# Tiled bias attention and a cosine-gated FFN: q and k transposed once in fp32, split into high and low halves afterwards

## The chip, the core and the metric

One core of a Trainium2 chip runs the whole program. The metric is device time in microseconds (us), the median of several executions. Engines are named as in the profile: PE is TensorE's matmul row and PEld its weight loads, DVE is VectorE, ACT is ScalarE, POOL is GpSimd, SP is SyncE, whose queue issues all DMAs.

## The reference

```python
scores = scale * np.matmul(q, k.transpose(0, 1, 3, 2))        # B=4, H=8, S=576, D=64
scores = scores + bias.transpose(2, 0, 1)[None]               # bias: a small MLP of log distances, per head
scores = scores - np.max(scores, axis=-1, keepdims=True)
attn = np.exp(scores); attn = attn / (attn.sum(-1, keepdims=True) + 1e-9)
x = np.matmul(attn, v)                                        # then (B*S, H*D) = (2304, 512)
h = x @ w_in; g = h * np.cos(h); out = g @ w_out              # d_ff = 2048
```

All is fp32. Products that need it are made of three fp32r matmuls, for which a matrix is split into a rounded high half and the low half that is left: high x high, high x low and low x high.

## The kernel before, in words

The program has three stages. The **bias stage** (to about 65 us) makes 36 groups of bias rows (`bias_hid`, `bias_rows`, `bias_store`) and stores them to DRAM, from where `load_bias` (L226) reads them back in tiles per head. The **attention stage** (to about 365 us) treats 16 units, a unit being a pair of heads of one batch element. The **FFN stage** takes the rest.

Order is written out by hand: `manual_schedule` keeps each engine's instructions in the order in which the Python code emits them, and the semaphores follow from the data. So an instruction that waits holds up all behind it on its engine.

A unit has five **slots** (`slot`, L551), one for each tile of 128 query rows (the fifth holds the last 64 rows of both heads). Slot j of a unit emits the scores of its tile (`qk`, L397: 12 fp32r matmuls, 6 in the fifth), for which two PSUM tiles (`ps_s`, two buffers, one for each head) are taken; DVE adds the bias and takes the minimum in one instruction (L419). The exponentials of the slot before are done on ACT (L437), their sums inverted on DVE (L449, L452) and the rows scaled by POOL (`norm`, L459). The tile of three slots ago is transposed on PE (L466, eight transposes; L471, one for the 64 left columns) and copied out of PSUM by ACT (first head) and DVE (second head). V's matmuls (`pv`, L514) of the unit before run in slots 0, 1, 3 and 4; their result is copied by ACT (L479) in slots 1 and 4.

**q and k of the next unit** are prepared beside that. `load` (L141) brings a pair of heads with one DMA for 512 rows (four successive rows, 1 KB, to a partition) and for k two more with the 64 rows left of k and of q. `split` (L169) makes the halves on POOL: one instruction for the high half (L176) and two for the low one (L179). `turn_main` (L188) transposes one half with four fp32r transposes (L191) into a PSUM bank and copies it on ACT (L198); `turn_left` (L205) does the 64 rows left of both halves with two transposes (L208) and four ACT copies (L211, L213). `T_EARLY` (L545) places them: k high in slot 0, k low in slot 1, the left rows and q high in slot 2, q low in slot 3, each between the scores and V's matmuls. All transposes take banks from one ring of three (`ps_t`, L380): a bank can be written again when the copy of what it held three requests ago is done. `POOL_PLAN` (L538) places the splits behind the norms of a slot, a unit or two ahead; `LOAD_PLAN` (L547) the loads; `W_PLAN` (L548) the FFN weights' conversion, a part of it in each second unit (DVE's L105 in slot 1, POOL's L109 in slot 2). For unit 0 the same is done in the bias stage (`T_FIRST`, L351, and the splits at n == 1).

Of the kernel before, what the change touches and what calls it, by code (L numbers as in the profile page):

```python
# [28 lines left out]
def kernel(  # L29
# [81 lines left out]
    with tc.manual_schedule():  # L111
# [21 lines left out]
        for t_ in qDs:  # L133
            nc.vector.memset(f(t_[0:64, :, 64:128]), 0.0)
            nc.vector.memset(f(t_[64:128, :, 0:64]), 0.0)

        vN = [vl.tile([128, 9, D], F32, name=f"vN{i}") for i in range(2)]

# [2 lines left out]
        def load(u, x):  # L141
            hp, b = units[u]
            src = {"q": q, "k": k, "v": v}[x]
            pair_ = src[b, 2 * hp : 2 * hp + 2]
            if x == "v":
                t = vN[u % 2]
                for h in range(2):
                    nc.sync.dma_start(
                        out=t[:, 4 * h : 4 * h + 4, :], in_=pair_[h, 0:512].rearrange("(c p) d -> p c d", p=128)
                    )  # L150
                for h in range(2):
                    nc.sync.dma_start(out=t[64 * h : 64 * h + 64, 8, :], in_=pair_[h, 512:576])
                return
            m = 5 if x == "k" else 4
            t = (lk if x == "k" else ld).tile([128, 2, m, D], F32, tag=x, name=f"n{x}")
            nc.sync.dma_start(
                out=t[:, :, 0:4].rearrange("p h r d -> p h (r d)"),
                in_=pair_[:, 0:512].rearrange("h (p r) d -> p h (r d)", r=4),
            )
            if x == "k":  # L160
                for i, o in ((k, 0), (q, 64)):
                    nc.sync.dma_start(
                        out=t[o : o + 64, :, 4], in_=i[b, 2 * hp : 2 * hp + 2, 512:576].rearrange("h p d -> p h d")
                    )
            nat[u, x] = t

        spl = {}

        def split(u, x, step=None):  # L169
            n = nat[u, x]  # L170
            m = n.shape[2]
            if step in (None, 0):
                spl[u, x] = sp.tile([128, 2, m, 128], F32R, tag=x, name=f"s{x}")
            hi, lo = (spl[u, x][:, a].rearrange("p c (h d) -> p h c d", h=2) for a in range(2))
            if step in (None, 0):
                nc.gpsimd.tensor_scalar(hi, n, 1.0, 1.0, ALU.mult, ALU.mult)  # L176
            for h in range(2):
                if step in (None, 1 + h):
                    nc.gpsimd.tensor_tensor(lo[:, h], n[:, h], f(hi[:, h]), ALU.subtract)  # L179
            if step in (None, 2):  # L180
                nat.pop((u, x))

        kN = {}

        def bank(dt=F32):
            return ps_t.tile([128, 512], dt, tag="t", name="pt")

        def turn_main(u, x, a):  # L188
            ps = bank(F32R)
            for c in range(4):  # L190
                nc.tensor.transpose(ps[:, 128 * c : 128 * c + 128], spl[u, x][:, a, c], identr)  # L191
            if x == "q":
                o = qTs[u % 2][:, a]
            else:
                if u not in kN:
                    kN[u] = tp.tile([128, 2, 640], F32R, tag="kN", name="kN")
                o = kN[u][:, a, 64:576]
            nc.scalar.activation(  # L198
                out=o.rearrange("p (x c) -> p x c", c=4),
                in_=f(ps).rearrange("p (c x) -> p x c", c=4),  # L200
                func=AF.Copy,
                scale=-0.125 if x == "q" else 1.0,
            )

        def turn_left(u):  # L205
            ps = bank(F32R)
            for a in range(2):
                nc.tensor.transpose(ps[:, 128 * a : 128 * a + 128], spl[u, "k"][:, a, 4], identr)  # L208
            i = f(ps)[:, 0:256].rearrange("p (a x) -> p a x", a=2)
            for o in (576, 0):  # L210
                nc.scalar.activation(out=kN[u][:, :, o : o + 64], in_=i[:, :, 0:64], func=AF.Copy)  # L211
            for r in (slice(0, 64), slice(64, 128)):
                nc.scalar.activation(out=qDs[u % 2][r, :, r], in_=i[r, :, 64:128], func=AF.Copy, scale=-0.125)  # L213

        def turn(u, ops):
            if u >= NU:
                return
            for op in ops:
                if op == "kx":
                    turn_left(u)  # L220
                else:
                    turn_main(u, op[0], "hl".index(op[1]))

        bias = {}

# [122 lines left out]
        for i in range(WPRE):  # L348
            W[i] = wpre[i]
        ACT_H = [k for k in range(36) if k % 4 != 3]  # L350
        T_FIRST = {11: ("kh",), 12: ("kl",), 13: ("kx",), 14: ("qh",), 15: ("ql",)}  # L351
        todo = [(t, gi) for t in (4, 0, 1, 2, 3) for gi in range(len(groups[t]))]
        held, hts = None, bias_hid(0)
        for n in range(len(todo) + 1):
            now = hts
            if n < len(todo):
                hts = bias_hid(n + 1) if n + 1 < len(todo) else None
                ps = bias_rows(n, now)
            if held:
# [6 lines left out]
            if n == 1:  # L366
                for x in "kq":
                    split(0, x)
            if n == 6:
                for x in "kq":  # L370
                    load(1, x)
            if n in T_FIRST:
                turn(0, T_FIRST[n])
            if n == 16:
                split(1, "k")
            if n == 20:
                load(2, "k")
        stage.close()
# [18 lines left out]
        def qk(u, j):  # L397
# [3 lines left out]
            for hf in range(2):  # L401
                for n, (a, b) in enumerate(((0, 0), (0, 1), (1, 0))):
                    for h in heads:
                        r = slice(64 * h, 64 * h + 64) if t < 4 else slice(0, 128)
                        o = HALF * hf + (64 if h == 0 else 0)
                        nc.tensor.matmul(  # L406
                            s[h][:, hf, 0:HALF],
                            qTs[u % 2][r, a, 128 * t : 128 * t + 128] if t < 4 else qDs[u % 2][:, a],
                            kN[u][r, b, o : o + HALF],
                            start=(n == 0),  # L410
                            stop=(n == 2),
                            tile_position=(r.start, 0),
                        )
# [100 lines left out]
        def pv(u, hf, chunks):  # L514
# [5 lines left out]
            for c in chunks:  # L520
                for h in range(2):
# [11 lines left out]
            if 4 in chunks:  # L533
                c0 = b * S + 256 * hf
                act_copy(xT[:, hp, c0 : c0 + WQ[hf]], X_.pop((u, hf))[:, 0 : WQ[hf]])
# [12 lines left out]
        W_PLAN = [("abs", 2), (0, 3), (0.5, 4), (1, 5), (2, 6), ("load", 6), (3, 7), (4, 7)]  # L548
        get = lambda i: jobs[i] if 0 <= i < len(jobs) else None

        def slot(i):  # L551
# [3 lines left out]
            if now:  # L555
                qk(u, j)
            if last:
                softmax_exp(*last, 0)
            turn(u + 1, T_EARLY[j])
            if last and len(heads(last)) == 2:  # L560
                softmax_exp(*last, 1)
            for du, hf, chunks in PV_EARLY[j]:
                if 0 <= u + du < NU:
                    pv(u + du, hf, chunks)
            if prev:
                if prev[1] in (0, 2):
                    alloc_half(prev[0], prev[1] // 2)
# [5 lines left out]
            if prev:  # L573
# [2 lines left out]
                    keep_main(*prev, 1, pt[1])  # L576
                else:
                    keep_both(prev[0], pt[0])
            if last:
                for h in heads(last):  # L580
                    norm(*last, h)
            if prev:
                keep_left(*prev, pl)
            if now:
                for du, x, step in POOL_PLAN[j]:
                    if u + du < NU:
                        split(u + du, x, step)
# [244 lines left out]
```

## Time and profile before

| | |
|---|---|
| time, median of 3 runs (lowest to highest) | 783.94 us (783.48 to 785.31) |
| profiled execution: time / span of its instructions | 785.39 us / 783.6 us |
| PE busy | 755.1 us, 96% |
| PEld busy | 603.7 us, 77% |
| DVE busy | 599.4 us, 76% |
| ACT busy | 465.4 us, 59% |
| POOL busy | 395.3 us, 50% |
| DMA | 58.57 MB in 58825 packets, 24.3% of 16 engines' span |

The busy shares are averages over three stages with different limits. The page's table of 40 slices shows PE at nine tenths or more nearly everywhere except in the first four slices (the bias stage and its end), and PE's granted clock at nine tenths or more but there. So the stage in which the change lies must be read slot by slot.

### The profile page before, as it was taken

The numbers are of one execution on the slowest core, as the hardware profiler recorded it, in microseconds if no ns is written. First come the engines' busy times: TensorE is split into PE (matmuls) and PEld (weight loads), VectorE is DVE, ScalarE is ACT, GpSimd is POOL, SyncE is SP. The second block draws the span as 40 slices with busy tenths as digits, with TensorE's granted clock in tenths as the row PEclk, the third lists the DMA queues.
The fourth block names the chain that finished last, engine by engine and source line by source line (L and its number), as shares of the span: only waits on it lengthen the run. The fifth ranks groups of instructions, "written<-read, shape, count | busy, mean of one in ns | idle before, by whom it ended". The sixth has DMA issues, their size and how long they took to land.

```text
span 783.6 us, 14808 instructions
## 1 busy us (share of the span) xinstructions
PE 755.1 (96%) x5338; PEld 603.7 (77%) x5338; DVE 599.4 (76%) x1309; ACT 465.4 (59%) x964; POOL 395.3 (50%) x486
## 2 busy tenths in 40 slices
PE   6988899999999999998999999999999999999997
PEld 2665676667666667666798989988888889899895
DVE  8973768687777777775468878899889898976655
ACT  5975677777777777785355555545454545443332
POOL 2201566676767666657345537455455464554400
PEclk9995899999999999999999999999999999999999
DMA  5775314422533161120010101111110101001112
GB/s 184 249 253 188 98 48 135 121 78 56 166 91 89 49 191 49 28 61 11 1 54 28 55 28 54 32 50 31 50 53 30 54 27 55 2 28 41 54 41 81
DMA packets 58825, 58.57 MB, mean 75 GB/s; under 512 B 28544, under 2 KB 45056, under 8 KB 58752
## 3 DMA queue, kind: packets, MB, share of 16 engines
q1 hardware_dynamic: 58752, 57.63, 24.3%
q8 instruction: 42, 0.69, 0.4%
q14 instruction: 31, 0.25, 0.1%
HBM read 42.00 MB, written 15.61 MB: 74 GB/s over the span
## 4 chain that ended last, share of the span: by engine, by line
PE 85%; DVE 6%; DMA 4%; ACT 2%; issue 2%; SPq 0%; DVEq 0%; ACTq 0%
PE ph L634 25%; PE po L689 24%; PE pv L524 12%; PE s L406 9%; PE pt L466 8%; PE pa L323 3%; PE pt L191 3%; DMA sc<-rt 2%; DVE P L419 1%; DVE ht L307 1%; PE pt L471 1%; DMA bt<-sc 1%; DVE PT L482 1%; DVE gl L663 1%; DVE acc L712 0%
## 5 line engine op out<-in xcount | busy, mean ns | idle before, releaser
L459 POOL TENSOR_SCALAR P<-P,rc 128x576 f32<-128x576 f32 x144 | 107.3, 756 | 112.7 <-ACT P L437 40.5
L638 ACT ACTIVATE a<-ph,quarter 128x384 int32<-128x384 f32 x96 | 55.6, 580 | 107.8 <-PE ph L634 107.0
L419 DVE CUSTOM_DVE_ANT_0 P<-s,bt 128x576 f32<-128x576 f32 x144 | 103.5, 751 | 20.6 <-PE s L406 13.7
L644 DVE SCALAR_TENSOR_TENSOR r<-a,ph 128x384 f32<-128x384 int32 x96 | 52.8, 550 | 79.5 <-ACT a L638 79.4
L437 ACT ACTIVATE P<-P,m 128x576 f32<-128x576 f32 x144 | 110.8, 771 | 2.6 <-DVE m L419 2.6
L509 POOL TENSOR_TENSOR xs<-xT,xs 128x384 fp32r<-128x384 f32 x96 | 107.2, 1116 | 8.0
L634 PE MATMUL ph<-xs,wpre 128*128 128x384 f32 x576 | 109.4, 338 | 0.8 <-DVE a L653 0.8
L634 PE MATMUL ph<-xs,w 128*128 128x384 f32 x576 | 108.3, 337 | 0.5 <-DVE a L653 0.5
L634 PEld LDWEIGHTS ph<-xs,wpre 128*128 128x128 f32 x576 | 101.8, 188 | 6.5 <-DVE a L653 2.1
L634 PEld LDWEIGHTS ph<-xs,w 128*128 128x128 f32 x576 | 101.4, 188 | 5.5 <-DVE a L653 1.4
L649 ACT ACTIVATE r<-r,hpi 128x384 f32<-128x384 f32 x96 | 59.3, 617 | 69.6 <-DVE r L645 69.6
L508 POOL TENSOR_SCALAR xs<-xT 128x384 fp32r<-128x384 f32 x96 | 61.6, 641 | 48.7 <-PE ph L634 48.7
L466 PEld LDWEIGHTS pt<-ident,P 128*128 128x128 f32 x576 | 62.9, 143 | 29.7 <-POOL P L459 13.7
L466 PE MATMUL pt<-ident,P 128*128 128x128 f32 x576 | 81.5, 283 | 2.3 <-DVE PT L482 2.3
L524 PE MATMUL pv<-PT,vN 128*64 128x320 f32 (+1 forms) x512 | 77.8, 424 | 2.6 <-ACT PT L479 2.4
L406 PE MATMUL s<-kN,qT 64*128 64x288 f32 x768 | 77.0, 323 | 2.8 <-DVE m L419 1.4
L689 PE MATMUL po<-w,gh 128*128 128x512 f32 x288 | 75.3, 396 | 0.0
L689 PE MATMUL po<-wpre,gh 128*128 128x512 f32 x288 | 75.2, 396 | 0.0
L663 DVE TENSOR_TENSOR gl<-a,gh 128x384 fp32r<-128x384 f32 x96 | 74.0, 771 | 0.6 <-ACT gh L657 0.6
L406 PEld LDWEIGHTS s<-kN,qT 64*128 64x128 f32 x768 | 59.0, 195 | 15.6 <-issue 7.5
L482 DVE COPY PT<-pt 128x512 f32<-128x512 f32 x64 | 43.9, 686 | 33.5 <-PE pt L466 33.5
L109 POOL TENSOR_TENSOR w<-wb,w 128x512 fp32r<-128x512 f32 x16 | 20.7, 1295 | 89.9 <-ACT w L107 89.9
(82 smaller groups left out, 1300.6 us busy)
## 6 DMA issues: line engine op xcount, KB each, us to landing
sc<-rt SPq DMA_DIRECT2D x36, 295.5 KB
raw<-in_moe_w_in_dram SPq DMA_DIRECT2D x16, 512.0 KB
raw<-in_moe_w_out_dram SPq DMA_DIRECT2D x16, 512.0 KB
bt<-sc SPq DMA_DIRECT2D x16, 288.0 KB
nk<-in_k_dram SPq DMA_DIRECT2D x16, 256.0 KB
nq<-in_q_dram SPq DMA_DIRECT2D x16, 256.0 KB
vN<-in_v_dram SPq DMA_DIRECT2D x32, 128.0 KB
bt<-sc SPq DMA_DIRECT2D x16, 256.0 KB
```

The source lines that it names most:

```text
L406: nc.tensor.matmul(s[h][:, hf, 0:HALF], qTs[u % 2][r, a, 128 * t : 128 * t + 128] if t < 4 else qDs[u % 2][:, a], kN[u][r, b, o : o + HALF ...
L419: nc.vector.tensor_tensor_reduce(neg.rearrange("p (a x) -> p a x", a=2), s[h][:, :, 0:HALF], bias[hp, t, h].rearrange("p (a x) -> p a x", ...
L437: nc.scalar.activation(out=P[u, j][:, 576 * h : 576 * h + 576], in_=neg, func=AF.Exp, bias=m[:, 0:1], scale=-1.0, accum_out=dn[u, j][:, h ...
L459: nc.gpsimd.tensor_scalar(p, p, r, 1.0, ALU.mult, ALU.mult)
L466: nc.tensor.transpose(ps[:, 128 * c : 128 * c + 128], p[:, o : o + 128], ident)
L508: nc.gpsimd.tensor_scalar(h, src, 1.0, 1.0, ALU.mult, ALU.mult)
L509: nc.gpsimd.tensor_tensor(l, src, f(h), ALU.subtract)
L524: nc.tensor.matmul(ps[64 * h : 64 * h + 64, 0 : WQ[hf]], a, m, start=(c == 0), stop=(c == 4), tile_position=(r.start, 64 * h), skip_group_ ...
L634: nc.tensor.matmul(ps, a, x, start=(i == 0), stop=(i == 3 * KD - 1))
L649: nc.scalar.activation(out=r, in_=r, func=AF.Sin, scale=SIN_SCALE, bias=hpi)
L663: nc.vector.tensor_tensor(gl, a, f(G[key][0]), ALU.subtract)
L689: nc.tensor.matmul(O[n][i], a[:, 128 * i : 128 * i + 128], w, start=(i0 == 0 and p == 0), stop=(i0 == GF - 1 and p == 2),)
```

## The change

- k and q are transposed as loaded, in fp32: four transposes and one ACT copy for each (512 rows), and one transpose with four copies for the 64 rows left of both. The copies go to SBUF tiles `turned["k"]` and `turned["q"]` of 640 columns; q is scaled and the two left blocks lie at columns 512 to 639 of q, with zeros beside them that are written once.
- POOL splits those: for each of k and q a high half of 640 columns (step 0) and two low halves of 320 columns (steps 1 and 2), written to where the scores read them. It follows the transposes, where it was ahead of them.
- The order in a slot: scores, both exponentials of the slot before, V's matmuls and ACT's copy of their result, the q/k transposes and their copies, P's transposes. k is turned in slot 0, the left rows in slot 1, q in slot 2. Splits come in slots 2 (k: steps 0 and 1 ahead of the norms, 2 behind), 3 (q: 0 ahead, 1 behind) and 4 (q: 2 ahead of the norms).
- The loads of q and k take one DMA for each head, and lay four rows of a head at a distance of two heads' width, so that the pieces are 256 bytes. q's load buffer is doubled, and the split halves' pool is gone; q is loaded two units ahead in slot 0, k three ahead in slot 2.
- For unit 0, k, the left rows and q are turned at n = 11, 12, 13 of the bias stage and split at 13 and 14; unit 1's k is split in unit 0's slots.

```diff
-        ld = opened(front, "ld", 1, "right")
+        ld = opened(front, "ld", 2, "right")
-        sp = opened(front, "sp", 1, "right")
...
-        qTs = [st.tile([128, 2, 512], F32R, name=f"qT{i}") for i in range(2)]
-        qDs = [st.tile([128, 2, 128], F32R, name=f"qD{i}") for i in range(2)]
...
+        qTs = [st.tile([128, 2, 640], F32R, name=f"qT{i}") for i in range(2)]
+        turned = {x: st.tile([128, 640], F32, name=f"{x}t") for x in "kq"}
...
-            t = (lk if x == "k" else ld).tile([128, 2, m, D], F32, tag=x, name=f"n{x}")
-            nc.sync.dma_start(
-                out=t[:, :, 0:4].rearrange("p h r d -> p h (r d)"),
-                in_=pair_[:, 0:512].rearrange("h (p r) d -> p h (r d)", r=4),
-            )
+            t = (lk if x == "k" else ld).tile([128, m, 2, D], F32, tag=x, name=f"n{x}")
+            for h in range(2):
+                nc.sync.dma_start(out=t[:, 0:4, h], in_=pair_[h, 0:512].rearrange("(p r) d -> p r d", r=4))
...
         def split(u, x, step=None):
+            n = turned[x]
...
             if step in (None, 0):
+                nc.gpsimd.tensor_scalar(o[:, 0], n, 1.0, 1.0, ALU.mult, ALU.mult)
+            for i in range(2):
+                c = slice(320 * i, 320 * i + 320)
+                if step in (None, 1 + i):
+                    nc.gpsimd.tensor_tensor(o[:, 1, c], n[:, c], f(o[:, 0, c]), ALU.subtract)
...
-                nc.tensor.transpose(ps[:, 128 * c : 128 * c + 128], spl[u, x][:, a, c], identr)
+                nc.tensor.transpose(ps[:, 128 * c : 128 * c + 128], n[:, c], ident)
...
+        def keep_turned(x, ps):
+            if x == "x":
+                o = turned["k"]
+                for at in (0, 576):
+                    nc.scalar.activation(out=o[:, at : at + 64], in_=ps[:, 0:64], func=AF.Copy)
+                for h in range(2):
+                    r = slice(64 * h, 64 * h + 64)
+                    nc.scalar.activation(
+                        out=turned["q"][r, 512 + 64 * h : 576 + 64 * h], in_=ps[r, 64:128], func=AF.Copy, scale=-0.125
+                    )
+                return
...
-        T_FIRST = {11: ("kh",), 12: ("kl",), 13: ("kx",), 14: ("qh",), 15: ("ql",)}
+        T_FIRST = {11: "k", 12: "x", 13: "q"}
+        S_FIRST = {13: "k", 14: "q"}
...
-            [(1, "q", 0), (1, "q", 1), (1, "q", 2)],
-            [],
-            [(2, "k", 0)],
-            [(2, "k", 1)],
-            [(2, "k", 2)],
+            ([], []),
+            ([], []),
+            ([("k", 0), ("k", 1)], [("k", 2)]),
+            ([("q", 0)], [("q", 1)]),
+            ([("q", 2)], []),
...
-        T_EARLY = [["kh"], ["kl"], ["kx", "qh"], ["ql"], []]
+        T_EARLY = ["k", "x", "q", None, None]
-        LOAD_PLAN = [[(3, "k")], [(2, "q")], [], [], [(1, "v")]]
+        LOAD_PLAN = [[(2, "q")], [], [(3, "k")], [], [(1, "v")]]
...
             if last:
-                softmax_exp(*last, 0)
-            turn(u + 1, T_EARLY[j])
-            if last and len(heads(last)) == 2:
-                softmax_exp(*last, 1)
+                for h in heads(last):
+                    softmax_exp(*last, h)
             for du, hf, chunks in PV_EARLY[j]:
                 if 0 <= u + du < NU:
                     pv(u + du, hf, chunks)
+                    if 4 in chunks:
+                        keep_x(u + du, hf)
+            if T_EARLY[j] and u + 1 < NU:
+                keep_turned(T_EARLY[j], turn(u + 1, T_EARLY[j]))
...
+            for x, step in POOL_PLAN[j][0]:
+                if u + 1 < NU:
+                    split(u + 1, x, step)
             if last:
                 for h in heads(last):
                     norm(*last, h)
             if prev:
                 keep_left(*prev, pl)
+            for x, step in POOL_PLAN[j][1]:
+                if u + 1 < NU:
+                    split(u + 1, x, step)
```

## Rows read from the trace of the kernel before

**Rows 1.** Stretches: us, busy us (count) of PE, PEld, DVE, ACT, POOL; PEclk, DMA share, GB/s.

```profile
40.00:65.00 25.00, 19.81 (x359) 12.76 (x350) 15.56 (x45) 16.91 (x26) 0.00 (x0) 0.88 0.78 265
...
100.00:150.00 50.00, 49.43 (x421) 34.35 (x419) 37.18 (x109) 37.13 (x92) 34.07 (x47) 1.00 0.41 118
```

**Rows 2.** PE's timeline of unit 4: start us, length us, engine, line, what, count.

```profile
139.91 1.05 PE L406 MATMUL s<-kN,qT 64*128 64x288 f32 x12
...
142.37 1.10 PE L466 MATMUL pt<-ident,P 128*128 128x128 f32 x8
...
143.51 1.06 PE L406 MATMUL s<-kN,qT 64*128 64x288 f32 x12
144.50 0.54 PE L191 MATMUL pt<-identr,sk 128*128 128x128 f32 x4
144.97 1.08 PE L524 MATMUL pv<-PT,vN 128*64 128x256 f32 x8
...
146.57 1.09 PE L466 MATMUL pt<-ident,P 128*128 128x128 f32 x8
...
147.70 1.06 PE L406 MATMUL s<-kN,qT 64*128 64x288 f32 x12
148.69 0.36 PE L208 MATMUL pt<-identr,sk 128*128 128x128 f32 x2
...
149.24 0.62 PE L466 MATMUL pt<-ident,P 128*128 128x128 f32 x4
150.03 0.33 PE L471 MATMUL pt<-ident,P 128*128 128x128 f32 x1 [0.16 <-ACT qD L213]
150.28 1.17 PE L406 MATMUL s<-kN,qT 64*128 64x288 f32 x12
151.38 0.54 PE L191 MATMUL pt<-identr,sq 128*128 128x128 f32 x4
151.89 1.30 PE L524 MATMUL pv<-PT,vN 128*64 128x320 f32 x8
...
154.08 1.03 PE L406 MATMUL s<-kN,qD 128*128 128x288 f32 x6
...
158.08 0.79 PE L406 MATMUL s<-kN,qT 64*128 64x288 f32 x8
```

**Rows 3.** ACT's timeline in slots 1 and 2 of unit 4.

```profile
146.71 0.38 ACT L479 ACTIVATE xT<-pv 128x256 f32<-128x256 f32 x1 [0.28 <-PE pv L524]
...
149.09 0.45 ACT L211 ACTIVATE kN<-pt 128x128 fp32r<-128x128 f32 x2 [0.48 <-PE pt L208]
...
150.00 0.60 ACT L198 ACTIVATE qT<-pt 128x512 fp32r<-128x512 f32 x1
```

**Rows 4.** DVE's timeline in slot 2 of unit 4: the second head's bias and minimum.

```profile
149.57 0.75 DVE L419 CUSTOM_DVE_ANT_0 P<-s,bt 128x576 f32<-128x576 f32 x1
```

**Rows 5.** The timeline of unit 3, slot 3: PE's weight load for the second head's scores.

```profile
132.26 0.82 PEld L406 LDWEIGHTS s<-kN,qT 64*128 64x128 f32 x11 [0.34 <-DVE m L419]
```

**Rows 6.** Groups by line and form on POOL, 100 to 340 us: busy us, mean ns | idle before.

```profile
L459 POOL TENSOR_SCALAR P<-P,rc 128x576 f32<-128x576 f32 x119 | 88.6, 756 | 63.9 <-PE pt L191 24.1 <-PE s L406 18.4 <-DVE rc L452 7.9
L179 POOL TENSOR_TENSOR sk<-nk,sk 128x320 fp32r<-128x320 f32 x26 | 23.5, 903 | 0.0
...
L109 POOL TENSOR_TENSOR wpre<-wb,wpre 128x512 fp32r<-128x512 f32 x7 | 9.0, 1293 | 0.0
L176 POOL TENSOR_SCALAR sk<-nk 128x640 fp32r<-128x640 f32 x12 | 8.7, 729 | 0.0
```

**Rows 7.** The timeline where unit 0 ends and unit 1 begins, POOL and PE.

```profile
82.22 1.63 POOL L459 TENSOR_SCALAR P<-P,rc 128x576 f32<-128x576 f32 x2 [3.26 <-DVE rc L452]
...
84.02 1.81 PE L406 MATMUL s<-kN,qT 64*128 64x288 f32 x12
```

**Rows 8.** Stretches as in rows 1: V's load lies in the first, q's in the second.

```profile
304.00:309.00 5.00, 5.00 (x48) 3.90 (x49) 4.00 (x12) 3.17 (x7) 3.40 (x6) 1.00 0.27 59
...
313.00:318.00 5.00, 4.72 (x45) 3.49 (x45) 4.29 (x14) 4.49 (x13) 1.92 (x4) 1.00 0.20 52
```

More of the change, by code (lines that the diff above doesn't have):

```diff
@@ L130 @@
         nc.vector.tensor_copy(identr, ident)
-        qTs = [st.tile([128, 2, 512], F32R, name=f"qT{i}") for i in range(2)]
-        qDs = [st.tile([128, 2, 128], F32R, name=f"qD{i}") for i in range(2)]
-        for t_ in qDs:
-            nc.vector.memset(f(t_[0:64, :, 64:128]), 0.0)
-            nc.vector.memset(f(t_[64:128, :, 0:64]), 0.0)
+        qTs = [st.tile([128, 2, 640], F32R, name=f"qT{i}") for i in range(2)]
+        turned = {x: st.tile([128, 640], F32, name=f"{x}t") for x in "kq"}
+        nc.vector.memset(turned["q"][0:64, 576:640], 0.0)
+        nc.vector.memset(turned["q"][64:128, 512:576], 0.0)
         vN = [vl.tile([128, 9, D], F32, name=f"vN{i}") for i in range(2)]
@@ L162, in load @@
                     nc.sync.dma_start(
-                        out=t[o : o + 64, :, 4], in_=i[b, 2 * hp : 2 * hp + 2, 512:576].rearrange("h p d -> p h d")
+                        out=t[o : o + 64, 4], in_=i[b, 2 * hp : 2 * hp + 2, 512:576].rearrange("h p d -> p h d")
                     )
             nat[u, x] = t
-        spl = {}
         def split(u, x, step=None):
-            n = nat[u, x]
-            m = n.shape[2]
-            if step in (None, 0):
[L173 to L181, printed above, removed]
+            n = turned[x]
+            if x == "k":
+                if u not in kN:
+                    kN[u] = tp.tile([128, 2, 640], F32R, tag="kN", name="kN")
+                o = kN[u]
+            else:
+                o = qTs[u % 2]
+            if step in (None, 0):
+                nc.gpsimd.tensor_scalar(o[:, 0], n, 1.0, 1.0, ALU.mult, ALU.mult)
[3 more added lines that the diff above has]
+                    nc.gpsimd.tensor_tensor(o[:, 1, c], n[:, c], f(o[:, 0, c]), ALU.subtract)
         kN = {}
@@ L186, in bank, with turn_main, turn_left @@
             return ps_t.tile([128, 512], dt, tag="t", name="pt")
-        def turn_main(u, x, a):
-            ps = bank(F32R)
+        def turn_main(u, x):
+            ps = bank()
+            n = nat[u, x].rearrange("p r h d -> p r (h d)")
             for c in range(4):
-                nc.tensor.transpose(ps[:, 128 * c : 128 * c + 128], spl[u, x][:, a, c], identr)
[L192 to L197, printed above, removed]
+                nc.tensor.transpose(ps[:, 128 * c : 128 * c + 128], n[:, c], ident)
+            return ps
+        def turn_left(u):
+            ps = bank()
+            nc.tensor.transpose(ps[:, 0:128], nat[u, "k"][:, 4].rearrange("p h d -> p (h d)"), ident)
+            return ps
+        def keep_turned(x, ps):
[9 more added lines that the diff above has]
+                return
+            o = turned[x][:, 64:576] if x == "k" else turned[x][:, 0:512]
             nc.scalar.activation(
                 out=o.rearrange("p (x c) -> p x c", c=4),
-                in_=f(ps).rearrange("p (c x) -> p x c", c=4),
+                in_=ps.rearrange("p (c x) -> p x c", c=4),
                 func=AF.Copy,
@@ L203, in turn_main, with turn @@
             )
[L205 to L222, printed above, removed]
+        def turn(u, x):
+            return turn_left(u) if x == "x" else turn_main(u, x)
         bias = {}
@@ L365 @@
             held = (n, ps)
-            if n == 1:
-                for x in "kq":
-                    split(0, x)
             if n == 6:
@@ L372 @@
             if n in T_FIRST:
-                turn(0, T_FIRST[n])
-            if n == 16:
-                split(1, "k")
+                keep_turned(T_FIRST[n], turn(0, T_FIRST[n]))
+            if n in S_FIRST:
+                split(0, S_FIRST[n])
             if n == 20:
@@ L407, in qk @@
                             s[h][:, hf, 0:HALF],
-                            qTs[u % 2][r, a, 128 * t : 128 * t + 128] if t < 4 else qDs[u % 2][:, a],
+                            qTs[u % 2][r, a, 128 * t : 128 * t + 128] if t < 4 else qTs[u % 2][:, a, 512:640],
                             kN[u][r, b, o : o + HALF],
@@ L583, in slot @@
                 keep_left(*prev, pl)
+            for x, step in POOL_PLAN[j][1]:
+                if u + 1 < NU:
+                    split(u + 1, x, step)
             if now:
-                for du, x, step in POOL_PLAN[j]:
-                    if u + du < NU:
-                        split(u + du, x, step)
                 for du, x in LOAD_PLAN[j]:
```

7 lines of the change are left out of this document (4 added, 3 removed).

## The prediction, made before the changed kernel ran

> **What bounds the kernel now.** I read the stretches first. From 100 to 340 us, over four such stretches, PE is busy in 99% of the time at full clock while DVE and ACT lie near 75% and POOL at 68% [rows 1]: PE sets the pace of the attention stage, and this is where q and k are turned. From 40 to 65 us PE has 19.8 of 25 us and DMA a share of 0.78 [rows 1]; there the chain of waits goes through stores to and loads from DRAM, so nothing is won there from a shorter PE. The FFN stage is untouched.
>
> Then I read PE's order in one unit [rows 2], since a busy PE can hide waits. Its slots start at 139.91, 143.51, 147.70, 150.28, 154.08 and 158.08: 3.60, 4.19, 2.58, 3.80, 4.00, in sum 18.17 us. Units with an even number repeat this; odd ones take 18.54, with all the difference in slot 3, where the second head's scores wait 0.34 for DVE [rows 5]. Unit 0 is held by DMAs and unit 15 turns nothing, so 14 units count.
>
> **The change part by part.** *The q/k transposes.* From the start of a group to the next group, k high and k low take 144.97 - 144.50 = 0.47 each, the left rows and q high 149.24 - 148.69 = 0.55, q low 151.89 - 151.38 = 0.51 [rows 2]: 2.00 us in a unit, of which a part is the switch to V's matmuls. A run of nine fp32 transposes of P takes 143.51 - 142.37 = 1.14, or 0.127 each [rows 2]; the new ones stand ahead of such a run and are of its kind, so nine of them cost 1.14 with no switch of their own. PE's own work falls by 0.86. How much of that reaches the end is seen slot by slot.
>
> *Slot 0:* -0.47 + 4 x 0.127 = +0.04. The copy of k (0.6, as in [rows 3]) can lie beside the eight transposes of P, so the ninth, which takes k's bank again, does not wait.
>
> *Slot 1:* -0.47 + 0.13 = -0.34, and a new wait. The left rows' bank is taken again by the ninth transpose of P, 9 x 0.127 = 1.14 behind them, and ACT's four copies must be done by then. ACT starts V's copy 146.71 - 146.57 = 0.14 behind the point where the left rows now begin; that is 0.38 long [rows 2, 3]; four copies took 150.00 - 149.09 = 0.91 [rows 3]. So they end at 1.43 at most and P waits 0.29. They are half as wide now; I take 0.25 (bounds 0 and 0.4). Slot 1: -0.09. Behind these copies on ACT stands the first head's copy of P, which has a slot's time.
>
> *Slot 2:* the same wait of the ninth transpose exists now, at 150.03 [rows 2], and goes, with 0.55 of transposes against 0.51. But the next slot's scores need the PSUM tile that DVE frees at 149.57 + 0.75 = 150.32 [rows 4], 2.62 behind the slot's start, fixed by the scores and two DVE instructions. A shorter PE waits for DVE instead. Slot 2: 0.
>
> *Slot 3:* q low goes with its switch, V's matmuls follow the scores: -0.51. The switch from scores to V is taken as long as that from scores to transposes (bounds -0.1 and +0.1). V needs ACT's copy of P from slot 2; from that slot's start to V 2.62 + 1.0 = 3.6 us pass, and ACT's share of 37.13 / 50 [rows 1] makes 2.7 of them: in time. *Slot 4:* nothing of it is changed on PE: 0. The sum for an even unit is +0.04 - 0.09 - 0.51 = -0.56.
>
> *Odd units:* the 0.34 comes from a weight conversion that DVE does at the end of slot 1, in front of slot 2's bias. The wait of 0.25 that is new in slot 1 gives DVE this time before slot 2 begins; I take 0.24 off (bounds 0 and 0.34), so -0.80.
>
> *Both exponentials ahead of V's copy* move ACT's waiting, not its work, which falls by two copies of 0.6. The cover is ACT's quarter of idle time.
>
> *POOL* now works between the transposes and the next unit's scores. Behind slot 2's start come k's three steps and q's three, 2 x (0.73 + 2 x 0.90) = 5.06, and two pairs of norms of 1.51 that stand ahead of q's last steps, 8.1 in all [rows 6]. I allow 0.3 for norms of slot 1 that run over and 0.7 for the reciprocals of slot 2 (an estimate, a little over the mean wait of a norm, 63.9 / 119 = 0.54 [rows 6]): end at 9.1. Slots 2 to 4 last 2.62 + 3.25 + 4.00 = 9.87. So it costs nothing by 0.8 us; in odd units 1.29 of L109 [rows 6] puts the end at 10.4, 0.5 late, but its last step writes columns that only slot 2 reads, and the step ahead of it ends in time. Bounds: 0, and 0.5 in seven units. Once it is not hidden: unit 0's last norms end at 83.85 and unit 1's scores begin at 84.02 [rows 7]; q's steps now stand behind, 0.9 for the first low half: +0.8 (bounds 0 and 1.7).
>
> *The loads.* One DMA more for each load, and 256-byte pieces. V's load is already of such pieces: share 0.27 for 59 GB/s, against 0.20 for 52 GB/s of q's 1 KB pieces [rows 8]; per byte 1.19 times, 0.2 us on a load of 256 KB. Where DMA is a limit, before 65 us, three such loads and three more issues lie; against that PE has one microsecond less to do there. Net 0, bounds -1 and +1. Elsewhere the share is 0.41 or less [rows 1] and loads come more than a unit ahead: 0.
>
> The Trainium skill (DMA: Bandwidth & Descriptors, Specifications) speaks against this part: below 512 bytes a transfer loses line rate to read-modify-write. By that, taken as double the time, an estimate, the three early loads would cost 3 us and the result would be 778.2; the trace's 1.19 decides.
>
> **Sum.** 7 x 0.56 + 7 x 0.80 = 9.5, less 0.8: 8.7 us. The profiled execution took 785.39 us, 1.45 over the median; from it 776.7, from the median 783.94 **775.2 us**, which I forecast.
>
> **The rivals.** *PE is all that counts.* If slot 2 follows PE and the bank wait does not come, each unit gains 0.86 plus the present wait in slot 2, 150.28 - 149.24 - 5 x 0.127 = 0.40 [rows 2]: 14 x 1.26 = 17.6, 766.3 us. For it: PE's 99%; against it: DVE's release at 150.32 stands 0.04 from PE's start. Chance 0.10.
>
> *A part is taken back by smaller waits.* If the scores need all of q's tile, odd units lose 0.5 and the start 0.9 more; if the four copies keep their width and the latency is counted, slot 1 loses 0.15 more: 3.5 + 0.9 + 2.1 = 6.5, 781.7 us at worst, about 779 for one of these. For it: the slack of 0.8 is small; against it: each wait alone is below it. Chance 0.17.
>
> *It is hidden anyway.* If DVE's pace decides slot 3 too, only the odd units' 0.24 is left, 1.7 us, and the start takes 0.8: 783, no change. DVE's 25% of idle time is against it. Chance 0.04.
>
> *POOL becomes the bound (slower).* Place: unit u+1's first scores wait for q's low halves. If each of the four norms ahead of q's last steps waits the mean of 0.54, 2.1 in place of 0.7, and the scores need the whole of q, the chain ends at 10.5 in even units and 11.8 in odd ones against 9.87: 0.65 and 1.9 late, on average 1.3. It decides from 0.62 on (8.7 / 14), and gives 783.94 - 8.7 + 14 x 1.3 = 793.4 us. For it: transposes now come ahead of the split. Against it: most of the norms' wait is for exponentials that now stand ahead of everything on ACT. Chance 0.06.
>
> *The clock.* PE's longest run of transposes grows from nine to thirteen. With four runs of nine in each unit the stretch has the clock at 1.00 [rows 1]. At half clock the scores took 1.81 for 1.06 [rows 2, 7]; if four slots of 14 units paid this 0.75, the time would be 817 us. Chance 0.01. The Trainium skill (TensorE: Matmul & The Clock Gate, Part 4) says that transposes do not count as PE activity for the clock; the trace's full clock beside 41 transposes of P in a unit has not shown that.
>
> **How the numbers follow.** The forecast has 0.62. Faster by over 0.2% (1.6 us, about what runs of this kernel can tell) are the forecast, PE alone and the smaller waits: 0.62 + 0.10 + 0.17 = 0.89; same 0.04; slower 0.06 + 0.01 = 0.07. The range takes in the bounds of the unknown terms: on the low side the odd units' 0.10 more (0.7), no wait in slot 1 (3.5), no loss at the start (0.8), 1 us at the front and half of slot 2's 0.40 (2.8) would be 8.8, and 1.6 of these are unlikely together: 768.0. On the high side 780.5 takes in any one of the smaller waits with the front's +1. About 0.17 is left out above, 0.04 below.
>
> **What would show it.** Right: slots of about 3.64, 4.10, 2.6, 3.3 and 4.0 us in even units; no transposes of q and k in slot 3; the ninth transpose of P in slot 1 waiting for ACT's copies; the first score matmuls of a unit not waiting for POOL except in unit 1; the FFN stage as long as before. Wrong: scores that wait for POOL in each unit, a slot 2 much under 2.5, a clock below 1.00 after 100 us, or stores of the bias stage landing later.

## The result, and the profile of the changed kernel

The changed kernel takes 770.8 us (median of 4 runs, 768.78 to 771.09) against 783.71 us (782.52 to 785.31): a ratio of 0.9828 [0.9804, 0.9853], 12.9 us less. The forecast was 775.2 us, 8.7 less; the time lies in its range. Two later measurements of the same order of work, told below, gave 0.9859 [0.9841, 0.9877] and 0.986 [0.9837, 0.9882], so the gain is 10 to 13 us (12.9, 11.3 and 10.0 by the medians). The profiled execution took 771.03 us, with a span of 769.2.

First two stretches of the profile, with the columns of [rows 1]: 100 to 150 us again, and 100 to 340 us, which is nearly all of units 2 to 14 and the scores of unit 15.

```profile
100.00:150.00 50.00, 49.40 (x409) 34.19 (x411) 37.72 (x114) 35.86 (x92) 35.74 (x48) 1.00 0.46 112
...
100.00:340.00 240.00, 235.62 (x1960) 162.94 (x1960) 181.46 (x549) 170.34 (x433) 172.49 (x227) 1.00 0.37 94
```

PE is busy 98% of the time from 100 to 340 us (237.18 of the 240 us before, 235.62 now) at a granted clock of 1.00 in both; what shrank is the unit. Unit 4 of the changed kernel on PE, to be laid beside [rows 2] (start, length, engine, line, what, count, wait before it):

```profile
137.68 1.06 PE L397 MATMUL s<-kN,qT 64*128 64x288 f32 x12
138.67 1.08 PE L515 MATMUL pv<-PT,vN 128*64 128x256 f32 x8
139.68 0.65 PE L515 MATMUL pv<-PX,vN 64*64 64x256 f32 x4
140.26 0.33 PE L192 MATMUL pt<-ident,nk 128*128 128x128 f32 x1
140.43 1.04 PE L457 MATMUL pt<-ident,P 128*128 128x128 f32 x8
141.40 0.33 PE L462 MATMUL pt<-ident,P 128*128 128x128 f32 x1
141.65 1.05 PE L397 MATMUL s<-kN,qT 64*128 64x288 f32 x12
142.64 0.65 PE L187 MATMUL pt<-ident,nq 128*128 128x128 f32 x4
143.13 0.60 PE L457 MATMUL pt<-ident,P 128*128 128x128 f32 x4
143.57 0.27 PE L462 MATMUL pt<-ident,P 128*128 128x128 f32 x1
143.77 0.39 PE L397 MATMUL s<-kN,qT 64*128 64x288 f32 x1
144.34 1.06 PE L397 MATMUL s<-kN,qT 64*128 64x288 f32 x11 [0.17 <-DVE m L410]
...
147.52 1.03 PE L397 MATMUL s<-kN,qT 128*128 128x288 f32 x6
...
151.53 1.05 PE L397 MATMUL s<-kN,qT 64*128 64x288 f32 x12
```

The slots, from one group of scores to the next, now are:

| us | slot 0 | 1 | 2 | 3 | 4 | unit |
|---|---|---|---|---|---|---|
| even, before | 3.60 | 4.19 | 2.58 | 3.80 | 4.00 | 18.17 |
| even, after | 3.66 | 3.97 | 2.12 | 3.75 | 4.01 | 17.51 |
| odd, before | 3.60 | 4.19 | 2.58 | 4.17 | 4.01 | 18.54 |
| odd, after | 3.66 | 3.97 | 2.12 | 3.80 | 4.01 | 17.56 |

An even unit gains 0.66 and an odd one 0.98, where 0.56 and 0.80 were forecast. One odd unit, unit 9, gains only 0.2 (18.34); it returns among the unexpected things.

Between the two profiled executions lie 785.39 - 771.03 = 14.4 us. From slot 1 of unit 1 (88.46 us before, 85.04 now) to the scores of unit 15 (341.69 and 327.65) the gain is 10.6 us; 3.4 us stand ahead of that, in the bias stage, unit 0 and the first slot of unit 1, and 0.3 behind. The 10.6 repeat in every profile of this program; the 3.4 do not: in two further profiles of it that slot began at 87.75 and 88.73 us, and in the kernel before and the three variants of it below it lay between 86.71 and 88.90. So the front scatters by 2 to 4 us between executions. The three measurements' gains of 12.9, 11.3 and 10.0 us average 11.4; less 10.6 and 0.3, about 0.5 us of that is the front's.

In front, POOL was idle where it had split unit 0's q and k. First the stretch from 6.4 to 11.7 us, of the kernel before, then of the changed one (columns as in [rows 1]):

```profile
6.40:11.70 5.30, 4.22 (x28) 1.18 (x28) 5.30 (x7) 0.63 (x2) 5.09 (x6) 1.00 0.82 250
```

```profile
6.40:11.70 5.30, 4.73 (x54) 2.70 (x58) 4.97 (x13) 1.91 (x4) 0.00 (x0) 1.00 0.80 210
```

DVE has 13 instructions in this stretch, where it had 7. The groups of DVE from 6.4 to 11.4 us (busy us, mean ns), before and after, show that it is one kind of instruction that became shorter:

```profile
L307 DVE TENSOR_SCALAR ht<-lt,edge 128x528 f32<-128x528 f32 x3 | 3.0, 1046 | 0.0
L307 DVE TENSOR_SCALAR ht<-lt,edge 128x544 f32<-128x544 f32 x3 | 2.6, 923 | 0.0
```

```profile
L300 DVE TENSOR_SCALAR ht<-lt,edge 128x544 f32<-128x544 f32 x3 | 1.3, 495 | 0.0
L300 DVE TENSOR_SCALAR ht<-lt,edge 128x528 f32<-128x528 f32 x3 | 1.3, 485 | 0.0
```

### The profile page after: what moved, and what is told of

The parts are those of the page before. It is cut to its first block, busy times and chain, and to the rows that moved or that the text cites. A ratio compares the mean times of both kernels' runs of the same rounds, so it can differ in the third digit from the quotient of the medians.

```text
span 769.2 us, 14541 instructions
## 1 busy us (share of the span) xinstructions
PE 739.5 (96%) x5194; PEld 593.3 (77%) x5194; DVE 590.0 (77%) x1307; ACT 442.1 (57%) x932; POOL 400.7 (52%) x486
## 3 DMA queue, kind: packets, MB, share of 16 engines
q1 hardware_dynamic: 83840, 57.63, 26.2%
## 4 chain that ended last, share of the span: by engine, by line
PE 85%; DVE 7%; DMA 3%; ACT 2%; issue 2%; SPq 1%; DVEq 0%; ACTq 0%
PE ph L632 26%; PE po L687 24%; PE pv L515 12%; PE s L397 9%; PE pt L457 8%; PE pa L316 3%; DVE P L410 3%; DMA sc<-rt 2%; PE pt L187 1%; PE pt L462 1%; ACT rt L331 1%; DVE PT L473 1%; DMA bt<-sc 1%; DVE gl L661 1%; DVE acc L710 1%
## 5 line engine op out<-in xcount | busy, mean ns | idle before, releaser
L397 PE MATMUL s<-kN,qT 64*128 64x288 f32 (+1 forms) x864 | 93.7, 316 | 8.5 <-DVE m L410 8.3
L397 PEld LDWEIGHTS s<-kN,qT 64*128 64x128 f32 (+1 forms) x864 | 71.0, 189 | 22.8 <-DVE m L410 16.0
L457 PEld LDWEIGHTS pt<-ident,P 128*128 128x128 f32 x576 | 65.2, 143 | 18.4 <-POOL P L450 11.2
```

Source lines behind the costliest of these rows:

```text
L397: nc.tensor.matmul(s[h][:, hf, 0:HALF], qTs[u % 2][r, a, 128 * t : 128 * t + 128] if t < 4 else qTs[u % 2][:, a, 512:640], kN[u][r, b, o : ...
L457: nc.tensor.transpose(ps[:, 128 * c : 128 * c + 128], p[:, o : o + 128], ident)
```

## The experiments

The first theory is that of the prediction: the gain lies on PE, in the transposes saved and in their place beside those of P. Each ratio below is to the kernel before, timed along with the run.

**The order alone.** The kernel before, with both exponentials and V's matmuls ahead of its old turns.

```diff
-                softmax_exp(*last, 0)
-            turn(u + 1, T_EARLY[j])
-            if last and len(heads(last)) == 2:
-                softmax_exp(*last, 1)
+                for h in heads(last):
+                    softmax_exp(*last, h)
...
+            turn(u + 1, T_EARLY[j])
```

> The kernel before with the new order alone: exponentials, V's matmuls, then the transposes of the split halves beside those of P. Theory A (the order and the single transposes share the gain): the switch from the halves' transposes to V goes in slots 0, 1 and 3, about 0.12 to 0.16 each, 0.40 a unit, 5.6 us: 778. Theory B (the halved transposes carry it all): 783.7. Theory C (the order carries most of it): under 775.

Measured: 779.25 us, 0.9953 [0.9937, 0.9969]. Even units last 17.86 (3.49, 4.06, 2.76, 3.53, 4.01), odd ones 18.33: the order is worth 0.31 and 0.21 us, about what Theory A had. In odd units DVE's weight conversion (L105) takes 1.04 us here against 0.90 in the kernel before, which goes with their smaller gain.

**The halved transposes alone.** The changed kernel, with q and k turned between the scores and V's matmuls, where they stood before.

```diff
+            if T_EARLY[j] and u + 1 < NU:
+                keep_turned(T_EARLY[j], turn(u + 1, T_EARLY[j]))
             for du, hf, chunks in PV_EARLY[j]:
...
-            if T_EARLY[j] and u + 1 < NU:
-                keep_turned(T_EARLY[j], turn(u + 1, T_EARLY[j]))
```

> The changed kernel with the q/k transposes put back between the scores and V's matmuls. Theory A: a switch of 0.18 more in slots 0 and 1, less the ninth transpose's wait for ACT of 0.06 to 0.1 there, 0.24 a unit: 774. Theory B, what counts is that the transposes stand beside those of P: 6 us or more lost, 777 and above.

Measured: 778.13 us, 0.993 [0.9913, 0.9947]. Even units last 17.57, only 0.06 more than in the changed kernel, all in slot 0: there the switch that the prediction counted costs next to nothing. (In slot 1 it is hidden: there the ninth transpose no longer waits for ACT, and the slot's length stays.) Odd units last 18.33, 0.77 more, of which 0.66 lies in slot 2. Its place is seen in the timelines of DVE, POOL and PE in unit 3:

```profile
129.61 1.25 DVE L105 SCALAR_TENSOR_TENSOR wb<-raw,wb 128x512 uint32<-128x512 uint32 x1
130.78 0.74 DVE L410 CUSTOM_DVE_ANT_0 P<-s,bt 128x576 f32<-128x576 f32 x1
```

```profile
129.59 0.73 POOL L172 TENSOR_SCALAR kN<-kt 128x640 fp32r<-128x640 f32 x1
```

```profile
131.59 0.40 PE L397 MATMUL s<-kN,qT 64*128 64x288 f32 x1 [0.60 <-DVE m L410]
```

and in those of DVE and POOL of the changed kernel at the same place:

```profile
124.74 0.68 DVE L105 SCALAR_TENSOR_TENSOR wb<-raw,wb 128x512 uint32<-128x512 uint32 x1
125.34 0.75 DVE L410 CUSTOM_DVE_ANT_0 P<-s,bt 128x576 f32<-128x576 f32 x1
```

```profile
124.78 1.24 POOL L172 TENSOR_SCALAR kN<-kt 128x640 fp32r<-128x640 f32 x1
```

The two instructions meet in both. Where DVE is 0.04 us ahead, it takes 0.68 and POOL 1.24; where POOL is 0.02 ahead, POOL takes 0.73 and DVE 1.25. DVE's bias for the scores stands behind L105, so only in the second case do the slot's first scores wait, 0.60. The time of 778.13 is that of Theory B, but the place beside P's transposes was worth only 0.06 a unit; the rest came from this meeting, which neither theory had. So the two halves of the change do not add: alone they gain 0.31 and 0.60 in an even unit (0.91 in sum, against 0.66 measured together), and 0.21 and 0.21 in an odd one (0.42, against 0.98), where the order also decides which engine is first.

**The loads alone.** The kernel before with the new loads, one DMA for each head in pieces of 256 bytes.

```diff
-            nc.sync.dma_start(
-                out=t[:, :, 0:4].rearrange("p h r d -> p h (r d)"),
-                in_=pair_[:, 0:512].rearrange("h (p r) d -> p h (r d)", r=4),
-            )
+            for h in range(2):
+                nc.sync.dma_start(out=t[:, 0:4, h], in_=pair_[h, 0:512].rearrange("(p r) d -> p r d", r=4))
```

> The kernel before with the new loads of q and k alone (one DMA for each head, pieces of 256 bytes). Theory A: 1.19 times the DMA time of such a load, hidden but for 0 to 0.6 us before 65 us: 784. Theory B, small pieces cost double: three early loads 3 us, 787.

Measured: 783.24 us, 1.0005 [0.9992, 1.0018]. The small pieces cost no time that can be measured, so the prediction's net of 0 for the loads holds. They do keep the DMA engines busy longer: the queue takes 25.6% of 16 engines' span where it took 24.3%, for the same 57.63 MB. That is 200.1 us of all 16 in place of 190.4, or 0.3 us more for each of the 32 loads, where the prediction took 0.2.

**POOL's early work put back.** The changed kernel, with six instructions of POOL at n == 1 as before, whose results nobody reads.

```diff
+            if n == 1:
+                for x, m in (("k", 640), ("q", 512)):
+                    i_ = nat[0, x].rearrange("p r h d -> p (r h d)")
+                    o_ = qTs[1]
+                    nc.gpsimd.tensor_scalar(o_[:, 0, 0:m], i_, 1.0, 1.0, ALU.mult, ALU.mult)
+                    for c in (slice(0, m // 2), slice(m // 2, m)):
+                        nc.gpsimd.tensor_tensor(o_[:, 1, c], i_[:, c], f(o_[:, 0, c]), ALU.subtract)
```

> The changed kernel with POOL's six instructions of the kernel before put back at n == 1 of the bias stage (same sizes, on the loaded q and k; their result is not used). Theory A, the front's gain of 3.8 us comes mostly from POOL no longer working beside DVE's first rows (984 ns a row beside POOL, 498 ns without): the first bias row is 1.5 us later, the sixth 2.5 us, and unit 1 begins 2 to 3 us later; time about 773. Theory B, the gain comes from the fewer transposes and copies on PE and ACT: rows and time as in the changed kernel, 770.8.

Measured: 773.85 us, 0.9883 [0.9865, 0.99]. The same stretch of its profile, and its first group of DVE from 6.4 to 11.4 us:

```profile
6.40:11.70 5.30, 4.13 (x28) 1.29 (x28) 5.22 (x7) 0.50 (x1) 4.93 (x6) 1.00 0.78 216
```

```profile
L300 DVE TENSOR_SCALAR ht<-lt,edge 128x528 f32<-128x528 f32 x3 | 3.0, 1037 | 0.0
```

DVE is back at 7 instructions, as Theory A had it, and ACT starts the first bias row at 12.38 us (12.10 before, 10.55 after), the seventh at 20.73 (20.62 and 18.12). That POOL slows DVE there is shown. What it is worth at the end of the bias stage is seen over all profiles. In the five with POOL's early work (this run, the kernel before and its three variants) the seventh bias row starts at 20.62 to 20.91 us and unit 0's scores at 64.08 to 65.14; in the eight without it, at 17.93 to 19.14 and 61.32 to 64.06. The means at unit 0 are 64.6 and 62.7, a difference of 1.9 us. At slot 1 of unit 1 the means still differ by 1.1 (88.3 and 87.2), but the two groups overlap. What is left of it in the program's time is not settled: this run is 3.0 us above the first measurement of the changed kernel, but 1.1 to 1.7 above the two later ones, which is within the front's scatter.

**Two that changed nothing.** S_FIRST at n = 26 and 27 in the changed kernel, and the early splits at n == 8 in the kernel before.

```diff
-        S_FIRST = {13: "k", 14: "q"}
+        S_FIRST = {26: "k", 27: "q"}
```

> The changed kernel with unit 0's splits on POOL at n == 26 and 27 of the bias stage in place of 13 and 14. Theory A, POOL beside DVE slows the bias rows wherever DVE is the limit: rows 14 to 24 come 1 us earlier, of which DMA waits leave 0 to 1: 770 to 770.8. Theory B, later POOL work costs nothing: 770.8.

```diff
-            if n == 1:
+            if n == 8:
                 for x in "kq":
                     split(0, x)
```

> The kernel before with unit 0's splits on POOL at n == 8 of the bias stage in place of 1. Theory A, POOL slows DVE only in the first rows, where nothing is yet in flight: rows 0 to 8 come 1.5 to 2.5 us earlier and 2 us reach the end, 781.5. Theory B, the contention only moves to later rows: the first rows earlier, rows 12 on as before, 783.5.

Measured: 772.79 us, 0.986 [0.9837, 0.9882], and 783.82 us, 1.0006 [0.9994, 1.0017]. POOL has nothing else in its queue there, so a later place in the program moves nothing: the splits ran as soon as their data were there, at 28.69 us (26.89 in the changed kernel) and at 6.70 (6.41 before). Neither tests what it was meant to; the first is in effect a third measurement of the changed kernel.

**The changed kernel once more**, with nothing altered.

> The changed kernel once more, as it stands, to see how its front varies: units 2 to 14 to 0.05 us as in its first profile (17.51 even, 17.56 odd); unit 1's second slot between 85 and 89 us; time 769 to 772.

Measured: 772.18 us, 0.9859 [0.9841, 0.9877]; every unit from 2 on as in the first profile, unit 9 included, and slot 1 of unit 1 at 87.75 us. That is as expected, but for a median 0.2 us above the expected times.

**How near POOL is.** The changed kernel, with q's first low half written twice (the same values).

```diff
-            ([("q", 0)], [("q", 1)]),
+            ([("q", 0)], [("q", 1), ("q", 1)]),
```

> The changed kernel with q's first low half made twice on POOL (0.88 us more in slot 3 of each unit; it writes the same values). Theory A: even units have 1.4 us of slack before the scores that need this half and lose nothing; odd units, where the weights' instruction of 1.3 us lies in the same chain, have 0.1 and lose about 0.8: 7 x 0.8 = 5.5, 776. Theory B, POOL has slack everywhere: 770.8. Theory C, the scores wait for all of q's tile: even units lose 0.4 too, 779.

Measured: 778.07 us, 0.9942 [0.9921, 0.9962]. POOL and PE where unit 4 of it begins:

```profile
135.96 2.64 POOL L176 TENSOR_TENSOR qT<-qt,qT 128x320 fp32r<-128x320 f32 x3
```

```profile
136.94 0.53 PE L397 MATMUL s<-kN,qT 64*128 64x288 f32 x4
137.83 0.80 PE L397 MATMUL s<-kN,qT 64*128 64x288 f32 x8 [0.37 <-POOL qT L176]
```

One step of 0.88 more delays the even units by 0.62 (slot 0 4.28 against 3.66), so only 0.26 of it found cover: it is in odd units, with the weights' conversion among POOL's work, that q's halves for the next unit are made. Odd units stay at 17.55, since the step found room in the even ones. That is Theory A, with 0.26 us of cover where it had 0.1. The rival in which POOL becomes the bound was a quarter of a microsecond away in every second unit.

**Filling the wait that is left.** In the changed kernel PE waits for DVE in each slot 3 (144.34 above). So V's left chunk of the first half moves from slot 1 to slot 2; in a second kernel the weights' last step on POOL moves as well.

```diff
-        PV_EARLY = [[(-1, 0, (0, 1))], [(-1, 0, (2, 3, 4))], [], [(-1, 1, (0, 1))], [(-1, 1, (2, 3, 4))]]
+        PV_EARLY = [[(-1, 0, (0, 1))], [(-1, 0, (2, 3))], [(-1, 0, (4,))], [(-1, 1, (0, 1))], [(-1, 1, (2, 3, 4))]]
```

> The changed kernel with V's last matmuls of the first half (0.58 us) and ACT's copy moved from slot 1 to slot 2, where the next scores wait 0.57 for DVE. Theory A: slot 1 shrinks by 0.6, slot 2 stays, POOL's chain then ends 0.5 later against the next unit, which odd units pay: 7 x 0.6 + 7 x 0.15 = 5 us less, 766. Theory B, DVE and ACT set the pace and not PE: 770 to 771.

```diff
-        W_PLAN = [("abs", 2), (0, 3), (0.5, 4), (1, 5), (2, 6), ("load", 6), (3, 7), (4, 7)]
+        W_PLAN = [("abs", 2), (0, 3), (0.5, 4), (1, 5), (2, 6), ("load", 6), (3, 7), (4, 9)]
```

> As the one before, and the weights' POOL instruction moved two slots later, behind the norms of slot 4, so that it stands ahead of no split. Theory A: odd units win 0.6 as well: 14 x 0.58 = 8 us less than the changed kernel, 763. Theory B, POOL was no limit in odd units: the same as the one before.

Measured: 765.72 us, 0.9779 [0.9762, 0.9795], and 765.41 us, 0.9772 [0.9758, 0.9787]. Even units fall to 16.91 (3.66, 3.35, 2.71, 3.18, 4.01), odd ones only to 17.47, with slot 3 at 3.74, in both kernels: POOL's step was not what held them. The first run's 766 was thus met with a wrong reason for the odd units, and of the second run's theories B holds. DVE, POOL and PE in unit 3 of the second show what did:

```profile
125.88 1.17 DVE L105 SCALAR_TENSOR_TENSOR wb<-raw,wb 128x512 uint32<-128x512 uint32 x1
126.97 0.74 DVE L410 CUSTOM_DVE_ANT_0 P<-s,bt 128x576 f32<-128x576 f32 x1
```

```profile
125.04 1.47 POOL L450 TENSOR_SCALAR P<-P,rc 128x576 f32<-128x576 f32 x2 [2.54 <-PE pt L457]
```

```profile
127.88 0.39 PE L397 MATMUL s<-kN,qT 64*128 64x288 f32 x1
128.46 0.81 PE L397 MATMUL s<-kN,qT 64*128 64x288 f32 x8 [0.18 <-DVE m L410]
```

Slot 1 is shorter, L105 begins behind a norm that POOL has under way, takes 1.17, and the bias comes late.

**Both together.** V's left chunk in slot 2, and the conversion's DVE step one slot later, with what follows it.

```diff
-        W_PLAN = [("abs", 2), (0, 3), (0.5, 4), (1, 5), (2, 6), ("load", 6), (3, 7), (4, 7)]
+        W_PLAN = [("abs", 2), (0, 3), (0.5, 4), (1, 5), (2, 7), ("load", 7), (3, 8), (4, 9)]
```

> The changed kernel with V's last matmuls of the first half in slot 2, the weights' third DVE instruction (1.17 us beside POOL in slot 2 of an odd unit) one slot later, behind slot 2's bias, and the steps after it one and two slots later. Theory A: in odd units the second head's scores of slot 3 no longer wait for DVE behind that instruction, 0.56 less: 7 x 0.56 = 3.9 us under the kernel with V alone moved (765.7), 762. Theory B, the wait only moves to slot 4: 765.5.

Measured: 761.57 us (761.13 to 764.31), 0.973 [0.9711, 0.9748], faster than both kernels. Odd and even units last 16.91. Its stretch from 100 to 340 us, and DVE and PE in unit 3:

```profile
100.00:340.00 240.00, 239.69 (x2024) 167.83 (x2020) 193.44 (x566) 176.33 (x443) 180.00 (x238) 1.00 0.39 94
```

```profile
126.23 1.09 DVE L105 SCALAR_TENSOR_TENSOR wb<-raw,wb 128x512 uint32<-128x512 uint32 x1
```

```profile
125.34 1.07 PE L397 MATMUL s<-kN,qT 64*128 64x288 f32 x12
```

L105 is still slow, but it now stands behind the bias of slot 2, and the twelve score matmuls run without a break, as Theory A had it. PE is busy 239.69 of 240 us, so in this stage no idle time of PE is left to fill.

## Why the prediction was right, and which terms were off

**The transposes.** Nine fp32 transposes ahead of P's were to cost 1.14 in place of 2.00. They do: from 142.64 to 143.13 four take 0.49, and the one for the left rows 0.17 (140.26 to 140.43), so nine take 2 x 0.49 + 0.17 = 1.15. Slot 0 was to grow by 0.04 and grew by 0.06.

**Slot 1: -0.09 forecast, -0.22 measured.** The ninth transpose of P does wait for ACT's copies: it begins at 141.40, when the last of them ends at 141.35. But the wait costs 0.12, not 0.25: the ten transposes of the slot take 141.65 - 140.26 = 1.39, where ten at 0.127 would take 1.27. ACT in slot 1 of unit 4, beside [rows 3]:

```profile
140.41 0.39 ACT L470 ACTIVATE xT<-pv 128x256 f32<-128x256 f32 x1 [1.04 <-PE pv L515]
140.69 0.33 ACT L199 ACTIVATE kt<-pt 128x64 f32<-128x64 f32 x2
140.90 0.45 ACT L202 ACTIVATE qt<-pt 64x64 f32<-64x64 f32 x2
141.37 0.60 ACT L470 ACTIVATE PT<-pt 128x512 f32<-128x512 f32 x1
```

The four copies, half as wide, end 140.90 + 0.45 - 140.69 = 0.66 after their start, against 0.91 of the wide ones, and they start 0.28 behind V's copy, where 0.38 was taken. The sign of the term, the wait and its cause were right; the step that was mis-sized is the copies, 0.25 by their length and 0.10 by their start. It makes 14 x 0.13 = 1.8 us.

**Slots 2 and 3: -0.51 forecast, -0.51 measured (even).** Here the reason was right to the tenth, though the slots are not those forecast: 2.12 and 3.75, where 2.6 and 3.3 were named. Slot 2 now ends at 2.12 by its first score matmul, since the first head's PSUM tile is free early; the second matmul waits for DVE and runs 144.34 - 141.65 = 2.69 after the slot's start, where 2.62 was forecast. DVE in slot 2 of unit 4, beside [rows 4]:

```profile
143.52 0.75 DVE L410 CUSTOM_DVE_ANT_0 P<-s,bt 128x576 f32<-128x576 f32 x1
```

So "a slot 2 much under 2.5", named as a mark against the forecast, was a bad mark: the start of the group hides the wait inside it. The rival in which PE alone counts falls with that wait, which the runs with V's left chunk in slot 2 then filled.

**Odd units: -0.80 forecast, -0.98 measured.** Of the 0.34 for DVE, 0.24 was to go, as slot 1's wait gives DVE time. Slots 2 and 3 of an odd unit were 0.37 longer than those of an even one and are 0.05 longer now. L105 begins 0.65 after slot 2's start (124.74 in unit 3, whose slot 2 starts at 124.09), where it began 0.81 after it (129.96, slot 2 at 129.15); that 0.16 is about the time that slot 1's wait gives to DVE. And it takes 0.68 where it took 0.90. Unit 3 of the kernel before, DVE and POOL:

```profile
129.96 0.90 DVE L105 SCALAR_TENSOR_TENSOR wb<-raw,wb 128x512 uint32<-128x512 uint32 x1
```

```profile
128.84 1.47 POOL L459 TENSOR_SCALAR P<-P,rc 128x576 f32<-128x576 f32 x2 [0.42 <-PE pt L466]
```

There it began while POOL's second norm had 0.36 to run (to 130.32); now that norm is all but over and POOL's split comes after it. That is the other 0.22. The step that was mis-sized took the wait as DVE's own work alone, and over half of it was POOL's.

**POOL's chain: end at 9.1 after slot 2's start in even units.** It ends at 151.04, 9.39 after:

```profile
149.17 1.87 POOL L176 TENSOR_TENSOR qT<-qt,qT 128x320 fp32r<-128x320 f32 x2
```

In odd units its end was forecast 0.5 late and its step ahead of that in time. Both hold: in unit 3 the last step ends 0.7 after the scores of unit 4 have begun, the one ahead of it 0.1 before them.

```profile
133.05 1.70 POOL L176 TENSOR_TENSOR qT<-qt,qT 128x320 fp32r<-128x320 f32 x2
```

**The start and the front: +0.8 and 0 forecast.** POOL's q steps do stand behind unit 0's late norms, and unit 1's scores wait for them, but 0.25 in place of 0.8: PE's weight loads and POOL at that place,

```profile
80.96 0.98 PEld L397 LDWEIGHTS s<-kN,qT 64*128 64x128 f32 x8 [0.25 <-POOL qT L176]
```

```profile
80.04 1.69 POOL L176 TENSOR_TENSOR qT<-qt,qT 128x320 fp32r<-128x320 f32 x2
```

since the high half, done earlier, lets the first matmuls go. Those twelve matmuls take 2.07 us, against 1.81 in [rows 7], both at a granted clock of 0.50 (80 to 82 us now, 84 to 86 before). For the bias stage the prediction weighed DMAs and PE, and not what POOL's leaving does to DVE, whose instruction takes half the time there. It put this at nothing, and it is worth 1.9 us where unit 0 begins. How much of that lasts, beside the front's scatter, is open.

**The loads, the clock and the rivals.** From unit 15's scores to the end it takes 441.6 us, against 441.9: the FFN stage is as long as before. The Trainium skill (DMA: Bandwidth & Descriptors, Specifications) has transfers under 512 bytes lose line rate; the estimate of 3 us from that did not show, with 1.0005 [0.9992, 1.0018] in the run of the loads alone; the queues were busy longer there, but in this kernel no time came of it, and the measurement decides. PE's granted clock is 1.00 from 100 to 340 us with thirteen transposes in a row, so the clock's rival falls; the Trainium skill (TensorE: Matmul & The Clock Gate, Part 4) says that for the clock transposes don't count as PE-busy in the same way, and the trace shows no loss from it here. Of the smaller waits none came in full, and nothing was hidden anyway: every slot forecast to shrink did. POOL did not become the bound, though it took only one step of 0.88 more to make it one in every second unit. One thing in the prediction's odds does not add up: PE alone, at 766.3 us, has a chance of 0.10, but only 0.04 is left below 768.0.

**Sum.** A gain of 9.5 was forecast for 14 units, and 10.6 came between slot 1 of unit 1 and unit 15, unit 9's 0.8 of loss included; for the start and the front a loss of 0.8 was forecast, and a gain of 0.5 on average, 3.4 in the profiled execution, came. The mechanism was right; slot 1's copies, the odd units' wait and the front were mis-sized, all to the same side. That slots 2 and 3 came out to the hundredth in sum is in part luck: the wait for DVE ended 2.69 after slot 2's start, 0.07 later than forecast, and from there to slot 4 it took 3.18, 0.07 less than the 3.25 forecast.

## What to carry to other kernels

Here a group of transposes placed beside others of its kind was worth mostly what its own instructions save, and less for the switch (0.06 us in slot 0 of the changed kernel, 0.11 with the split halves of the kernel before); its order mattered more by what then met on the other engines. When work moves from one place of GpSimd's queue to another, price VectorE's instructions on SBUF at both places, since here the two held each other up by nearly a whole instruction. And where a wait for one engine stays in an otherwise full one, look for a piece of work without a due time that fits in: here 0.58 us of V's matmuls, moved by one slot, and one conversion step moved behind the bias, gave 10.6 us more (772.18 to 761.57).

## What the runs showed of the hardware that was not expected

VectorE's fp32 TENSOR_SCALAR of some 540 columns in SBUF took 485 to 495 ns alone and 923 to 1046 beside GpSimd. With two SBUF inputs (L105) it took 0.68 when it began first and 0.90 to 1.25 when GpSimd had begun 0.02 to 0.39 us ahead, and GpSimd's split 0.73 or 1.24 in the same way. How much longer the later one took follows what the earlier one still had to run: L105 grew by 0.22 where 0.36 was left (the kernel before), by 0.41 where 0.56 was left (both edits), by 0.49 with 0.63 (the kernel with the weights' POOL step moved too) and by 0.57 with 0.71 (transposes first). In each it is what was left less 0.14 or 0.15, and with 0.08 left (the changed kernel) L105 did not grow. The Trainium skill (GPSIMD Engine Reference, Specifications) says that GpSimd shares its SBUF interfaces with VectorE, with contention where a VectorE instruction is in a two-port mode or reads two SBUF inputs; the two-input L105 agrees, with these numbers. Whether the one-input TENSOR_SCALAR runs in such a mode, no run here shows.

Unit 9 is longer by 0.8 us in each of three profiles of the changed program. Its slot 2 is the same meeting, lost by 0.07 us:

```profile
230.22 1.20 DVE L105 SCALAR_TENSOR_TENSOR wb<-raw,wb 128x512 uint32<-128x512 uint32 x1
```

```profile
230.15 0.72 POOL L172 TENSOR_SCALAR kN<-kt 128x640 fp32r<-128x640 f32 x1
```

What starts it is 0.27 us in slot 0, where ACT takes up the copy of k 0.37 after PE's transposes end by the record:

```profile
224.68 0.60 ACT L207 ACTIVATE kt<-pt 128x512 f32<-128x512 f32 x1 [2.11 <-PE pt L187]
```

In the kernel with both edits unit 9 keeps these 0.28 and nothing more. Their cause was not tried and stays open.
